# A spectral filter and a gated MLP on one core: real filter copied on chip, two row groups transposed by DMA, one input batch loaded in quarters

## The chip, the core and the metric

The kernel runs on one core of one Trainium2 chip. The time is the device time of one execution in microseconds; of several executions the median is given. A core has five engines with an instruction queue each: TensorE (PE, whose weight loads are listed as PEld), VectorE (DVE), ScalarE (ACT), GpSimd (POOL) and SyncE (SP). SyncE here does nothing but issue DMA transfers; GpSimd issues the loads of inputs and also computes. Matmuls write to PSUM, and another engine must copy ("evacuate") the result to SBUF before TensorE can use it again.

## What is computed

```python
X = np.fft.rfft(x, axis=1)              # x: 8 x 3008 x 256
Y = X * (filt_r + 1j * filt_i)[None]    # filters: 1505 x 256
y = np.fft.irfft(Y, n=3008, axis=1)
t = y.reshape(8 * 3008, 256)
h = t @ w_in                            # 256 -> 2048
g = h * sigmoid(beta * h)
out = g @ w_out                         # 2048 -> 256
```

A convolution along the sequence of each of eight batches, by Fourier transform, and then a two-layer network with a gated activation on all 24064 tokens. Inputs and output are float32; the kernel works in bfloat16 between them.

## The kernel before

The transform of length 3008 = 47 x 64 is done by matmuls with tables of sines and cosines, in four steps. Step 1 (`s1`, L628; for batch 0 `first1`, L305) transforms over the 47; `a` is its result. A transposition brings `a` into the tile `a2`. Step 2 (`s23`, L661) transforms over the 64, the spectrum is multiplied with the filter (L672 to L677, p_t, q_t and their sum v_t), and step 3 (L687) transforms back over the 64; the result `z` goes through DRAM (L692, L699) into tiles `zz` with the 96 rows in partitions. Step 4 (`last4`, L557) transforms back over the 47 and gives `y`. Batches 1 to 7 do all this with DMA transposes for `a2` (`a2_read`, L648: eight instructions of 128 x 768 on SyncE).

Batch 0 goes first, alone, in a stage of some 36 us in which the tables are made as well. There the filter is held doubled: `fri` has the real part in partitions 0 to 63 and the imaginary part in 64 to 127. `product(i)` makes two products for two frequencies, `inverse3(i)` runs two iterations behind it: eight matmuls into the PSUM tile `psz` (L477), evacuated into `z_t`. `z_t` holds 32 columns j in four groups of eight. Group 0 is transposed at once (L592), put through `last_z` (step 4 of batch 0), and the main stage begins. Groups 1 to 3 are transposed inside the main stage by `turn_z` (L549, eight transposes on TensorE into `pz`, then one evacuation into `zz`), two units for a group.

The main stage is a loop over 47 blocks of 512 tokens by 16 slices of the hidden layer, 752 steps. A step multiplies with a slice of w_in (L852, two matmuls of 512 columns into `hps`), has ScalarE evaluate the activation (L867) and, two steps later, multiplies with w_out (L907, four matmuls of 256 columns into `acc`). After 16 steps the block is copied from `acc` to `ost` and stored.

The Fourier work of the later batches, and the rest of batch 0, is strewn over these steps. The order is written by hand: `place(a, z, units)` spreads a list of small functions evenly over the steps a to z; at each step the functions placed there are emitted between its L852 and its L907 matmuls. Each engine and each DMA queue then works in that order. The lists that matter here are `uz(g)` (turn_z and last_z of group g), `u1(b)` (step 1), `u23(b)` (steps 2 and 3; 15 units, step 3 three units behind step 2), `u4(b)` (step 4), `ut` (a sign change of a table), `ux(b)` (load of a batch's x on the GpSimd queue) and `uf(a, z)`.

`uf` loads the filter's real part a second time, into both halves of `frr`, with 12 transfers on the SyncE queue: batches 1 to 7 multiply p_t with `frr` and q_t with the upper half of `fri`. The tile `frr` can't be filled earlier in its upper 16 rows of frequencies, because w_out is staged there (`load_wout`, L146) until `scale_wout` (L153, GpSimd) has brought it into `wout_sb`.

There are three PSUM pools: `hpsum` (two buffers), `opsum` and `fpsum` (three each). A PSUM tile's matmuls wait until the evacuation of the buffer's earlier content is done. `xpool` has one buffer, so the x of a batch can be loaded only after step 1 of the batch before.

Of the kernel before, what the change touches and what calls it, by code (L numbers as in the profile page):

```python
# [9 lines left out]
P = 128  # L10
# [3 lines left out]
F32 = mybir.dt.float32  # L14
BF16 = mybir.dt.bfloat16
# [11 lines left out]
M = 64  # L27
H = M // 2
NK = 24
J = 32  # L30
KG = 6
NG = NK // KG
JG = 8
NJG = J // JG
# [5 lines left out]
def kernel(  # L40
# [10 lines left out]
    nc = tc.nc  # L51
# [71 lines left out]

    X_WHOLE = [(0, 80, 0, J), (80, NP, 0, J)]
    X_HALVES = [(0, 80, 0, J // 2), (80, NP, 0, J // 2), (0, 80, J // 2, J), (80, NP, J // 2, J)]
    X_FIRST = [(0, 80, 0, JG), (80, NP, 0, JG), (0, 80, JG, 2 * JG), (80, NP, JG, J)]
    X_FIRST += [(0, 80, g * JG, (g + 1) * JG) for g in range(2, NJG)]

# [290 lines left out]
    xs = {}  # L419
# [14 lines left out]
    for go in tabs[::-1]:  # L434
        go()

    z_t = ypool.tile([P, NDC, J, KP], BF16, name="z_t", tag="y")
    pq = {}

    def product(i):  # L440
# [22 lines left out]
    def inverse3(i):  # L463
        k0 = 2 * i
        p_t, q_t = pq.pop(i)

        last = i == NK // 2 - 1
        for j0, j1 in ((0, JG), (JG, J)) if last else ((0, J),):
            nj = 4 * (j1 - j0)
            if j0:  # L470
                ps = fpsum.tile([P, 2, NDC, nj], F32, name="psz", tag="f")
            else:
                ps = opsum.tile([P, 2, NDC, nj], F32, name="psz", tag="acc")
            for src, tab in ((p_t, t3), (q_t, t3b)):
                for e in range(2):
                    for dc in range(NDC):
                        nc.tensor.matmul(  # L477
                            ps[:, e, dc, :],
                            lhsT=src[:, e, dc * P : (dc + 1) * P],
                            rhs=tab[:, k0 + e, 4 * j0 : 4 * j1],  # L480
                            start=src is p_t and dc == 0 and e == 0,
                            stop=src is q_t,
                            skip_group_check=True,
                        )
            for e in range(2) if last else (None,):
                if last:
                    dst = z_t[:, :, j0:j1, 4 * (k0 + e) : 4 * (k0 + e) + 4]
                    src = ps[:, e].rearrange("p c (j a) -> p c j a", a=4)
                else:
                    dst = z_t[:, :, :, 4 * k0 : 4 * k0 + 8].rearrange(  # L490
                        "p c j (e a) -> p e (c j) a", e=2
                    )
                    src = ps.rearrange("p e c (j a) -> p e (c j) a", a=4)
                evac(dst, src, not last or j0 > 0)

    def table4():
        for src, dst in ((t1b, t4b), (t1, t4)):
# [7 lines left out]
    for i in range(NK // 2 + FLAG):  # L505
# [24 lines left out]
        if i >= FLAG:  # L530
            inverse3(i - FLAG)

    for i in range(4):
        scale_wout(i)

    ys = {}
    ys[0] = ypool.tile([P, NDC, NK * P], BF16, name="y", tag="y")
    zz0 = {}
    zz0[0] = apool.tile([P, NK * P], BF16, name="zz", tag="a1")
    zz0[0] = zz0[0][:KP, : JG * D].rearrange("p (j d) -> p j d", j=JG)  # L540


    def turn_z(g, i, on_act=False):
        if g not in zz0:
            zz0[g] = zzpool.tile([KP, JG, D], BF16, name="zz", tag="zz")
        pz = fpsum.tile([P, 4, D], BF16, name="pz", tag="f")
        for e in range(4):
            for dc in range(NDC):
                nc.tensor.transpose(  # L549
                    pz[:KP, e, dc * P : (dc + 1) * P], z_t[:, dc, JG * g + 4 * i + e, :], ident[:]  # L550
                )
        evac(zz0[g][:, 4 * i : 4 * i + 4, :], pz[:KP], on_act)

    def last4(zz, tab, jj, dc, dst, on_act, own=None, first=NP):
        ps = own or fpsum.tile([P, 4, P], F32, name="ps4", tag="f")
        for e in range(4):
            nc.tensor.matmul(  # L557
                ps[:, e, :NP],
                lhsT=zz[:, jj + e, dc * P : (dc + 1) * P],
                rhs=tab[:],  # L560
                start=True,
                stop=True,
            )
        rest = []
        for n0, n1 in ((0, NP),) if own is None or first == NP else ((0, first), (first, NP)):
            rest.append(
                lambda n0=n0, n1=n1: evac(
                    dst[:, n0:n1],
                    ps[:, :, n0:n1].rearrange("p j n -> p n j"),
                    on_act,  # L570
                    inv_scale,
                )
            )
        rest.pop(0)()
        return rest
# [8 lines left out]

    for i in range(4):
        if i % 2:
            pz = opsum.tile([P, 2, D], BF16, name="pz", tag="acc")
        else:
            pz = fpsum.tile([P, 2, D], BF16, name="pz", tag="f")
        for e in range(2):  # L590
            for dc in range(NDC):
                nc.tensor.transpose(  # L592
                    pz[:KP, e, dc * P : (dc + 1) * P], z_t[:, dc, 2 * i + e, :], ident[:]
                )
        evac(zz0[0][:, 2 * i : 2 * i + 2, :], pz[:KP], i % 2 == 1)
    pw[0] = hpsum.tile([P, TB], F32, name="pw", tag="hps")
    warm(1)
    rest = []
# [23 lines left out]

    def s1(b, i, on_act):
        s = st[b]
        jq, dc = divmod(i, NDC) if b == 1 else divmod(i, J // 4)[::-1]
        ps = fpsum.tile([P, 4, P], F32, name="ps1", tag="f")
        for e in range(4):
            nc.tensor.matmul(  # L628
                ps[:, e, :KP],
                lhsT=s["x"][:, 4 * jq + e, dc * P : (dc + 1) * P],  # L630
                rhs=t1b[:],
                start=True,
                stop=True,
            )
        dst = s["a1"][dc].rearrange("p (k j a) -> p j k a", j=J, a=4)
        evac(
            dst[:, 4 * jq : 4 * jq + 4],
            ps[:, :, :KP].rearrange("p j (k a) -> p j k a", a=4),
            on_act,
        )  # L640
# [53 lines left out]
    def zz_read(b):  # L694
        s = st[b]
        s["zz"] = []
        for h in range(NJG):
            t = zzpool.tile([KP, JG, D], BF16, name="zz", tag="zz")
            nc.sync.dma_start(t[:], s["d2r"][:, h * JG : (h + 1) * JG, :])  # L699
            s["zz"].append(t)  # L700

    def s4(b, i, on_act):
# [37 lines left out]
    def u23(b):  # L740
        return [lambda i=i: s23(b, i) for i in range(NK // 2 + VLAG)]
# [2 lines left out]
        return [lambda i=i: s4(b, i, act and i % 2 == 1) for i in range(J // 2)]  # L744

    def uz(g, act=False):
        return [lambda i=i: turn_z(g, i) for i in range(2)] + [
            lambda i=i: last_z(g, i, act) for i in range(2 * NDC)
        ]

    def uf(a, z):
        return [
            go
            for k0 in range(a, z, JG)
            for at in (0, M)
            for go in load_filter(frr, filt_r, at, k0, JG, nc.sync)
        ]


    def ut(n):  # L760
# [4 lines left out]
            for k in range(0, NK, NK // n)  # L765
        ]

    def ux(b):
        def go():
            xs[b] = load_x(b, X_WHOLE)  # L770

        return [go]

    place(0, 0, rest, per=9)
    place(1, 14, uz(1, True))
    place(15, 29, uz(2, True))
    units = uz(3, True)
    place(20, 24, units[:2], per=2)
    place(34, 58, units[2:])

    first_step = [(S * b // TB) * NFB for b in range(B + 1)]
    if B > 1:
        units = u1(1, True)
        place(3, 8, units[: J // 4], per=2)
        place(10, 10, uf(0, JG), per=9)
        at = place(9, 14, units[J // 4 :], per=9)
        place(at + 1, at + 1, [lambda: a2_read(1)] + uf(JG, NK), per=9)
        place(14, 20, ut(4), per=2)
        units = u23(1)
        place(20, 53, units[: NK // 2], per=2)  # L790
        at = place(55, 58, units[NK // 2 :], per=2)
        assert at < 60
        place(60, 60, [lambda: zz_read(1)], per=9)
        place(67, 79, u4(1), per=2)
    if B > 2:
        place(36, 36, ux(2), per=9)
        at = place(52, 66, u1(2, True), per=3)
        assert at < 75
        place(75, 75, [lambda: a2_read(2)], per=9)
    for b in range(2, B):  # L800
# [38 lines left out]
    for s in range(len(steps) + LAG):  # L839
# [34 lines left out]
        if s >= LAG:  # L874
# [40 lines left out]
            if fb == NFB - 1:  # L915
                for h, a in enumerate(acc):
                    if h * per % 2 == 0:
                        ost = ostp.tile([P, 2, D], F32, name="ost", tag="ost")
                    c = h * per % 2
                    on_act = h == 0 and i < 6 or last and h == 0  # L920
                    if last and h == nch - 1:
                        for half in range(2):
                            cols = slice(half * P, (half + 1) * P)
                            evac(ost[:, c : c + per, cols], a[:, :, cols], half == 1)
                    else:
                        evac(ost[:, c : c + per, :], a[:], on_act)
                    store(t0 + h * per * P, per * P, ost[:, c : c + per, :])


# [28 lines left out]
```

## Time and profile before

| what | value |
|---|---|
| median of 5 runs | 776.81 us (776.61 to 779.73) |
| the profiled execution | 776.79 us |
| its span | 775.0 us |
| TensorE busy | 766.6 us |
| ScalarE busy | 595.5 us |
| VectorE busy | 378.9 us |
| GpSimd busy | 142.9 us |
| step 0's first L852 matmul starts at | 36.5 us |

The span is the time from the first to the last instruction in the trace; the device time is 1.8 us longer. Lines begin with the line number of the kernel where that is meant; in a line of instructions "out<-in" names the tile written and the tiles read, with partitions x elements and type. After the bar in a row of a group come its total busy time, the mean of one in ns, and the idle time of the engine just before, with what ended it. "xN" counts instructions. A queue's rows end in q (SPq).

### The profile page before, as it was taken

What the parts mean: (1) busy time and instruction counts of PE and PEld (TensorE: products, weight loads), DVE (VectorE), ACT (ScalarE), POOL (GpSimd) and SP (SyncE); (2) the same over time, 40 slices, a digit from 0 to 9 for tenths busy, and PEclk for the clock granted to TensorE, in tenths of its full rate; (3) what the DMA queues carried; (4) which work ended last, traced back from release to release, by engine and by line L of the source; (5) the groups of instructions that cost most, each with busy time, mean ns of one, the idle gap of its engine ahead of it and who ended that gap; (6) DMA issues with size and microseconds to landing.
All of it is one profiled execution on the core that took longest, in us unless ns stands there. A gap on an engine that the chain in (4) does not pass through costs nothing.

```text
span 775.0 us, 16219 instructions
## 1 busy us (share of the span) xinstructions
PE 766.6 (99%) x6444; PEld 553.8 (71%) x6444; DVE 378.9 (49%) x641; ACT 595.5 (77%) x926; POOL 142.9 (18%) x145
## 2 busy tenths in 40 slices
PE   8999999999999999999999999999999999999998
PEld 4877777777777777877778777787777776776665
DVE  7836846645446553474526735277353761401001
ACT  7888887886678867787677876778767787677776
POOL 7523401420013100231002410034000430000000
PEclk9999999999999999999999999999999999999999
DMA  7969755516911268022861237512451114100101
GB/s 177 237 159 195 167 162 112 135 49 156 175 43 69 92 142 161 30 92 80 157 134 50 75 120 142 106 66 78 130 110 55 49 69 129 56 28 28 55 28 55
DMA packets 103291, 80.48 MB, mean 104 GB/s; under 512 B 48466, under 2 KB 96996, under 8 KB 102258
## 3 DMA queue, kind: packets, MB, share of 16 engines
q1 hardware_dynamic: 100496, 63.73, 30.5%
q0 software_dynamic: 2720, 15.73, 10.6%
q8 instruction: 50, 0.82, 0.4%
q14 instruction: 25, 0.20, 0.1%
HBM read 46.15 MB, written 35.65 MB: 106 GB/s over the span
## 4 chain that ended last, share of the span: by engine, by line
PE 97%; ACT 1%; DMA 1%; DVE 0%; POOL 0%; issue 0%; POOLq 0%; DVEq 0%
PE acc L907 42%; PE hps L852 42%; PE ps L557 3%; PE ps L628 3%; PE ps L687 2%; PE ps L661 2%; DMA xg<-in_x_dram 1%; PE psz L477 1%; PE pz L549 0%; ACT a L109 0%; ACT a_t L109 0%; PE pb L403 0%; POOL xg L120 0%; PE ps L451 0%; PE ps2q L451 0%
## 5 line engine op out<-in xcount | busy, mean ns | idle before, releaser
L867 ACT ACTIVATE gT<-hps,beta_sb 128x512 bf16<-128x512 f32 x752 | 516.5, 688 | 166.5 <-PE hps L852 154.9
L907 PE MATMUL acc<-wout_sb,gT 128*128 128x256 bf16 x3008 | 451.5, 272 | 0.0
L852 PE MATMUL hps<-y,win_sb 128*128 128x512 bf16 (+8 forms) x1730 | 447.7, 351 | 0.0
L907 PEld LDWEIGHTS <-gT 128*128 128x128 bf16 x3008 | 279.6, 98 | 106.3 <-ACT gT L867 0.2
L852 PEld LDWEIGHTS <-win_sb 128*128 128x128 bf16 x1730 | 165.0, 98 | 24.4 <-issue 0.2
L677 POOL TENSOR_TENSOR v_t<-p_t,q_t 128x512 bf16<-128x512 f32 x84 | 106.8, 1271 | 383.9 <-DVE q_t L676 375.3
L111 DVE COPY ost<-acc 128x512 f32<-128x512 f32 (+2 forms) x89 | 56.6, 675 | 194.1 <-PE acc L907 188.4
L111 DVE CAST a<-ps 128x384 bf16<-128x384 f32 x96 | 53.5, 558 | 91.5 <-PE ps L628 91.4
L113 DVE TENSOR_SCALAR y<-ps 128x376 bf16<-128x376 f32 (+1 forms) x115 | 61.7, 545 | 59.5 <-PE ps L557 59.5
L672 DVE TENSOR_TENSOR p_t<-ps,frr 128x512 f32<-128x512 f32 x84 | 58.1, 692 | 33.4 <-PE ps L661 30.9
L676 DVE TENSOR_TENSOR q_t<-ps,fri 64x512 f32<-64x512 f32 x84 | 58.3, 694 | 1.2
L673 DVE SCALAR_TENSOR_TENSOR q_t<-ps,fri 64x512 f32<-64x512 f32 x84 | 57.4, 684 | 1.1
L557 PEld LDWEIGHTS <-zz 96*128 96x128 bf16 x512 | 35.3, 97 | 29.1 <-issue 0.3
L109 ACT ACTIVATE z<-ps 128x512 bf16<-128x512 f32 x84 | 49.7, 591 | 0.0
L628 PEld LDWEIGHTS <-xg 94*128 94x128 bf16 x448 | 30.7, 97 | 23.6 <-issue 0.6
L628 PE MATMUL ps<-t1b,xg 94*128 94x96 bf16 x448 | 36.7, 205 | 0.1
L557 PE MATMUL ps<-t,zz 96*128 96x94 bf16 x448 | 36.7, 204 | 0.0
L661 PE MATMUL ps<-a,t 128*128 128x256 bf16 x168 | 32.1, 273 | 0.0
L687 PE MATMUL ps<-v_t,t 128*128 128x256 bf16 x168 | 32.1, 273 | 0.0
L120 POOL DMA_DIRECT2D xg<-in_x_dram x22 | 12.1, 552 | 98.0 <-PE acc L907 93.9
L661 PEld LDWEIGHTS <-t 128*128 128x128 bf16 x168 | 15.7, 98 | 14.1
L687 PEld LDWEIGHTS <-t 128*128 128x128 bf16 x168 | 16.3, 98 | 6.4 <-DVE q_t L676 0.4
(118 smaller groups left out, 192.7 us busy)
## 6 DMA issues: line engine op xcount, KB each, us to landing
out_dram<-ost SPq DMA_DIRECT2D x80, 256.0 KB
d<-z SPq DMA_DIRECT2D x28, 384.0 KB
zz<-d SPq DMA_DIRECT2D x28, 384.0 KB
xg<-in_x_dram POOLq DMA_DIRECT2D x6, 1280.0 KB, 10.2
frr<-in_filt_r_dram SPq DMA_DIRECT2D x12, 256.0 KB
out_dram<-ost SPq DMA_DIRECT2D x20, 128.0 KB
frr<-in_moe_w_out_dram POOLq DMA_DIRECT2D x4, 512.0 KB, 13.0
xg<-in_x_dram POOLq DMA_DIRECT2D x6, 224.0 KB, 11.1
```

The lines of the kernel that those rows point to most:

```text
L111: nc.vector.tensor_copy(dst, src)
L113: nc.vector.tensor_scalar_mul(dst, src, scale)
L557: nc.tensor.matmul(ps[:, e, :NP], lhsT=zz[:, jj + e, dc * P : (dc + 1) * P], rhs=tab[:], start=True, stop=True,)
L628: nc.tensor.matmul(ps[:, e, :KP], lhsT=s["x"][:, 4 * jq + e, dc * P : (dc + 1) * P], rhs=t1b[:], start=True, stop=True,)
L661: nc.tensor.matmul(ps[:, e, :], lhsT=t2[:, k0 + e, 3:5, :].rearrange("p c k -> p (c k)"), rhs=s["a2"][g][:, :, kk + e, :], start=True, sto ...
L672: nc.vector.tensor_tensor(p_t[:], ps[:], frr[:, ks_, :], ALU.mult)
L676: nc.vector.tensor_tensor(q_t[:M], ps[M:P], fri[M:P, ks_, :], ALU.mult)
L677: nc.gpsimd.tensor_tensor(v_t[:], p_t[:], q_t[:], ALU.add)
L687: nc.tensor.matmul(ps[:, e, :], lhsT=t3[:, k0 + e, :], rhs=v_t[:, e, :], start=True, stop=True)
L852: nc.tensor.matmul(hps[:, pos - t0 : pos - t0 + ln], lhsT=win_sb[:, dc, fb * P : (fb + 1) * P], rhs=ys[b][:, dc, n0 : n0 + ln], start=(dc ...
L867: nc.scalar.activation(gT[:, :tn], hps[:, :tn], ACT.Silu, scale=beta_sb[:, fb : fb + 1])
L907: nc.tensor.matmul(acc[tb // per][:, tb % per, :], lhsT=g_[:, tb * P : (tb + 1) * P], rhs=wout_sb[:, f_, :], start=(f_ == 0 and tb % per = ...
```

## The change

- The upper half's copy of the real filter no longer comes from DRAM. GpSimd copies `fri[:64]` into both halves of `frr`, eight frequencies at a time (`double`): four copies behind `scale_wout`, two at steps 24 and 29. `uf` and its 12 transfers are gone.
- `z_t` is split. Group 0 has a tile of its own, `z_0`; groups 1 to 3 are in `z_t` in the order group, column half, j, row, with the rows padded from 96 to 128 by zeros. `inverse3` evacuates both pieces, so ten of the evacuations on ScalarE become two each.
- Groups 2 and 3 are turned by `read_z`: one DMA transpose each, of 128 x 2048, on the SyncE queue at step 9. Group 1 keeps `turn_z`, with its two evacuations on ScalarE instead of VectorE. `zz` tiles are laid out by column half first. The last_z units of groups 2 and 3 stand at steps 17 to 29 and 36 to 56.
- The x of batch 2 is loaded in quarters (two transfers each) at steps 29 to 41, not whole at step 36; step 1 of batch 2 stands at steps 56 to 69 instead of 52 to 66, in the order of batch 1.
- The last 128 tokens: each half of the columns gets a tile of its own and its own store, one issued by SyncE and one by ScalarE.

```diff
-    z_t = ypool.tile([P, NDC, J, KP], BF16, name="z_t", tag="y")
+    z_0 = a2pool.tile([P, NDC, JG, KP], BF16, name="z_0", tag="a2")
+    z_t = ypool.tile([P, NJG - 1, NDC, JG, P], BF16, name="z_t", tag="y")
+    gp.memset(z_t[:, :, :, :, KP:], 0.0)
...
-            for e in range(2) if last else (None,):
-                if last:
-                    dst = z_t[:, :, j0:j1, 4 * (k0 + e) : 4 * (k0 + e) + 4]
-                    src = ps[:, e].rearrange("p c (j a) -> p c j a", a=4)
-                else:
...
-                evac(dst, src, not last or j0 > 0)
+            for e0, ne in ((0, 1), (1, 1)) if last else ((0, 2),):
+                cols = slice(4 * (k0 + e0), 4 * (k0 + e0 + ne))
+                if j0 == 0:
+                    evac(
+                        z_0[:, :, :, cols].rearrange("p c j (e a) -> p e (c j) a", a=4),
+                        ps[:, e0 : e0 + ne, 0].rearrange("p e c (j a) -> p e (c j) a", a=4),
+                        not last,
+                    )
+                if j1 == J:
+                    evac(
+                        z_t[:, :, :, :, cols].rearrange("p g c j (e a) -> p e (g c j) a", a=4),
...
+    def double(k0, at):
+        gp.tensor_copy(frr[at : at + M, k0 : k0 + JG, :], fri[:M, k0 : k0 + JG, :])
+
     for i in range(4):
         scale_wout(i)
+    for k0 in (0, JG):
+        for at in (0, M):
+            double(k0, at)
...
+    def read_z(g):
+        zz0[g] = zzpool.tile([P, NDC, JG, P], BF16, name="zz", tag="zz")
+        nc.sync.dma_start_transpose(
+            zz0[g].rearrange("p c j d -> p (c j) d"),
+            z_t[:, g - 1].rearrange("p c j r -> p (c j r)"),
+        )
...
-        jq, dc = divmod(i, NDC) if b == 1 else divmod(i, J // 4)[::-1]
+        jq, dc = divmod(i, NDC) if b < 3 else divmod(i, J // 4)[::-1]
...
-    place(1, 14, uz(1, True))
-    place(15, 29, uz(2, True))
-    units = uz(3, True)
-    place(20, 24, units[:2], per=2)
-    place(34, 58, units[2:])
+    place(9, 9, [lambda: read_z(2), lambda: read_z(3)], per=9)
+    place(1, 14, [lambda i=i: turn_z(1, i, True) for i in range(2)] + uz(1, True))
+    place(17, 29, uz(2, True))
+    place(36, 56, uz(3))
...
-        place(10, 10, uf(0, JG), per=9)
         at = place(9, 14, units[J // 4 :], per=9)
-        place(at + 1, at + 1, [lambda: a2_read(1)] + uf(JG, NK), per=9)
+        place(at + 1, at + 1, [lambda: a2_read(1)], per=9)
         place(14, 20, ut(4), per=2)
+        place(24, 29, [lambda at=at: double(2 * JG, at) for at in (0, M)], per=9)
...
-        place(36, 36, ux(2), per=9)
-        at = place(52, 66, u1(2, True), per=3)
+        place(29, 41, ux(2, X_QUARTERS), per=9)
+        at = place(56, 69, u1(2, True), per=3)
...
-                        for half in range(2):
+                        for half, eng in ((0, nc.sync), (1, nc.scalar)):
                             cols = slice(half * P, (half + 1) * P)
-                            evac(ost[:, c : c + per, cols], a[:, :, cols], half == 1)
-                    else:
-                        evac(ost[:, c : c + per, :], a[:], on_act)
+                            ost = pqpool.tile([P, 2, D], F32, name="ost", tag="pq"[half] + "_t")
+                            evac(ost[:, :1, :P], a[:, :, cols], half == 1)
+                            eng.dma_start(out[TOK - P :, cols], ost[:, 0, :P])
+                        continue
+                    evac(ost[:, c : c + per, :], a[:], on_act)
```

## The prediction

> **What bounds the kernel now.** I read the page's head first, then its chain of waits.
>
> ```profile
> span 775.0 us, 16219 instructions
> PE 766.6 (99%) x6444; PEld 553.8 (71%) x6444; DVE 378.9 (49%) x641; ACT 595.5 (77%) x926; POOL 142.9 (18%) x145
> PE 97%; ACT 1%; DMA 1%; DVE 0%; POOL 0%; issue 0%; POOLq 0%; DVEq 0%
> ```
>
> TensorE is busy 766.6 of 775.0 us and is 97% of the chain that ended last. So a deleted TensorE instruction shortens the run by its own spacing, and everything done on other engines is free until TensorE has to wait for it. I then read the chain in order of time where the change acts (start, length, what).
>
> ```profile
> 53.69 0.43 PE hps L852 x2
> 54.12 0.45 PE pz L549 x8
> 54.57 0.44 PE acc L907 x4
> ...
> 56.30 0.45 PE pz L549 x8
> ...
> 58.92 0.43 PE hps L852 x2
> 59.52 0.45 PE pz L549 x8
> ...
> 64.05 0.45 PE pz L549 x8
> ```
>
> The transposes of batch 0's groups 2 and 3 (turn_z, L549) stand in the chain itself, 0.45 us for a unit of 8. A step without extra work is 0.43 + 0.44 = 0.87 us.
>
> Third, the stretch before step 0, 5 us at a time (columns: stretch, length, then busy us and count of PE, PEld, DVE, ACT, POOL, the granted clock, DMA share, GB/s):
>
> ```profile
> 20.00:25.00 5.00, 4.90 (x73) 4.71 (x73) 4.22 (x8) 4.83 (x9) 2.64 (x6) 1.00 1.02 231
> 25.00:30.00 5.00, 5.00 (x74) 4.59 (x72) 5.00 (x10) 4.21 (x8) 3.58 (x6) 1.00 1.04 172
> ```
>
> Here PE, DVE and ACT are all nearly full: no engine has much to give. Fourth, the waits of the Sync queue and the rows of its transfers:
>
> ```profile
> 46.29 0.23 SPq L521 DMA_DIRECT2D mark<-xg  x1
> ...
> 52.66 12.04 SPq L648 DMA_TRANSPOSE a<-a  x8
> ...
> L648 SPq DMA_TRANSPOSE a<-a x56: 1210/1287/6620, 52.7 to 578.4; - x56
> ```
>
> The second is the reading of batch 1's a2 by DMA transposes; the third gives least, median and most ns of one such instruction over all batches.
>
> **The change part by part.**
>
> *Transposes removed from TensorE.* In the instruction order 32 transposes with their weight loads are gone: turn_z of groups 2 and 3, four units. 4 x 0.45 = **-1.8 us**, all on the path. Their four evacuations of 0.69 us leave VectorE, which was not on the path.
>
> *DMA transposes in their place.* Two instructions on Sync, each of 128 x 2048 elements, 16 blocks of 128 x 128. No row has this size. The nearest, L648, moves 6 blocks in 1.21 to 1.29 us: 0.213 us a block, 16 x 0.213 = 3.4 us each, 6.8 us for both. Group 2 is first used in step 17 (about 57 us), group 3 in step 36. The Trainium skill speaks against this: "VectorE: DVE Perf Modes", section "The three transpose paths", puts a 128 x 128 bf16 block at 390 ns on TensorE and 1309 ns by the DMA crossbar. By that, one instruction is 16 x 1.309 = 20.9 us, both 41.9 us, and batch 1's transposes, behind them on the queue, would be some 35 us late: a run near 810 us. The row is of the same operation on the same queue and gives a sixth of that price per block when blocks share an instruction (and TensorE's block costs 0.056 us in the chain, not 0.39), so I take the row.
>
> What is queued behind them decides. Sync issues them after the mark (46.29 + 0.23 = 46.52), so they end at 46.5 + 6.8 = 53.3. Batch 1's eight transposes began at 52.66 and now begin at 53.3. The first two make the tile that the first L661 matmul reads: 53.3 + 2 x 1.28 = 55.9, and the transfer share falls to 0.00 within about 0.9 us of the last issue of such a group (125.1, batch 2), so it lands near 56.8. TensorE reaches that matmul in step 20, one step number earlier than before: 58.92 + 0.43 - 2 x 0.45 (two units gone by then) + 0.17 (one last_z unit now ahead of it) = 58.6. Margin 1.8 us. Each group of eight has one instruction of about 2.0 to 2.3 us, 1 us over the median; two such would use the margin up. I put +0.1 us here, from 0 to 5 (the upper end below, as a rival). The rows near 6.6 us come from stretches where an x load runs beside them; between 46.5 and 56 none is left, since the filter loads are gone.
>
> *Filter reload removed.* 12 Sync transfers of 256 KB and their issue go (4 before the transposes, 8 after at 64.88 to 68.7); output stores behind them move up by 4 us. TensorE waited for none of this: 0 us.
>
> *GpSimd copies.* Six of 64 x 2048 f32. Not in the trace. By element, the bf16 copy L293 (768 in 0.83 us) gives 2.2 us, the multiplication L153 (1024 in 1.89 us) 3.8 us; I take 3, nearer to a copy. Four run after the last L153 (44.27 + 1.89 = 46.2) and end at 55 to 61.4; the first v_t was at 63.28. The other two stand between v_t adds from step 24 on and delay one by at most 3.8 us, with 8 us before its matmul. 0 us, hidden behind the steps' matmuls. If the first four exceed (69.4 - 1.3 - 46.2) / 4 = 5.5 us each, the first L687 matmul at 69.40 waits, 4 us for each us more. VectorE is under 60% busy there, so VectorE slowed by the copies would stay covered.
>
> *More instructions on ScalarE before step 0.* z_t is split: each of the ten whole evacuations in inverse3 becomes two, of 128 and 384 elements. Rows:
>
> ```profile
> L109 ACT ACTIVATE z_t<-psz 128x512 bf16<-128x512 f32 x11 | 6.4, 595 | 1.2 <-PE psz L477 1.2
> L109 ACT ACTIVATE a<-ps 128x384 bf16<-128x384 f32 x16 | 7.9, 492 | 0.0
> L109 ACT ACTIVATE t<-pt 128x128 bf16<-128x128 bf16 x1 | 0.3, 273 | 0.0
> ```
>
> 492 + 273 - 595 = 170 ns by durations, but instructions overlap: starts lie 0.51 us apart behind a 512, 0.37 behind a 384, 0.16 to 0.22 behind a 128, so +0.02 to +0.08. "VectorE: DVE Perf Modes", section "The TRN2 errata", has a fixed 172 cycles at 1.2 GHz for a PSUM source, 143 ns a split: 0.86 us over the six iterations in which ScalarE also evacuates a table or an a2. By the row it is 0.1 to 0.5, which pushes back the full TensorE and VectorE behind it. Against it, group 0's transposes now wait for the small piece of the last evacuations, not the whole (0.51 + 0.595 against 0.57 + 0.275: 0.26 us sooner). Net **+0.15**, between -0.2 and +0.9. The z_t memset on GpSimd (1536 elements, up to 1.7 us) falls into a wait of 1.78 us for a filter load.
>
> *Group 1's evacuations go to ScalarE.* Two of 96 x 1024, about 1.05 us by the slope of the rows, near 38.6 and 40.7. ScalarE had a gap of 1.38 us before the silu of step 4. The psum buffer of the second comes free at about 41.8, and the matmuls that need it stood at 42.1. 0 us, at most +0.3.
>
> *Batch 2's x in quarters and its later s1.* Eight GpSimd issues of 0.55 us instead of two, +3.3 us on an engine that is 18% busy; they land before step 56. s1 has the same 64 matmuls, moved among full steps: 0 us.
>
> *The last store.* Both halves get tiles of their own and two queues. The profile's tail is:
>
> ```profile
> 771.35 0.29 DVE L111 COPY ost<-acc 128x128 f32<-128x128 f32 x1 [0.34 <-PE acc L907]
> 771.67 0.28 ACT L109 ACTIVATE ost<-acc 128x128 f32<-128x128 f32 x1 [1.14 <-DVE ost L111]
> ...
> 771.98 0.41 SPq L812 DMA_DIRECT2D out_dram<-ost  x1
> ```
>
> ScalarE's half still waits for VectorE's in the new order, so its store is issued at 772.0 as before; only 64 KB less follow it. **-0.1**, from +0.1 to -0.4.
>
> Sum: -1.8 + 0.1 + 0.15 - 0.1 = -1.65 us. The profiled execution took 776.79 us (span 775.0 and 1.8 around it), the median of five is 776.81, so the sum carries over: 776.81 - 1.65 = **775.2 us**.
>
> **The rivals.**
> 1. *Small gain, as summed*, 774.5 to 776.5: chance 0.57. That is under 0.3% (2.3 us), about what a measurement tells from no change.
> 2. *Nothing is lost*: split free, 0.26 us earlier into step 0, tail at its best: -1.8 - 0.2 - 0.4 = -2.4, 774.4 us; with transposes a little dearer than 0.45 (a wait or a buffer that goes with them) 774.0. For it: PE never waits for long. Against: ScalarE is full at 20 to 25 us. Chance 0.22.
> 3. *The wait for a2 takes the place of the transposes*, slower. Place: the first L661 matmul in step 20, in-order on TensorE. If the pair of DMA transposes takes more than 6.8 + 1.8 = 8.6 us, each further us is one us of run; from 10.3 us (5.1 each) on the kernel is slower than before. At the 6.62 us of the longest row, 13.2 us, the stall is 4.6: 776.8 - 1.7 + 4.6 = 779.7. For it: sixteen blocks in one instruction are not in the trace, and rows of up to 6.62 us for six blocks are. Chance 0.15, of which 0.13 clearly slower.
> 4. *GpSimd copies too slow*: at 7 us each the first L687 waits 6 us, 781 us. Against: both nearby rows. Chance 0.05.
> 5. *The change doesn't do what it says*: no effect, 776.8. Nearly excluded, since the deleted units are in the chain. 0.01.
>
> **How the numbers follow.** Faster by over 0.3% (below 774.5): rival 2, 0.22. Slower by over 0.3% (above 779.1): 0.13 of rival 3 and rival 4, 0.18. The rest, 0.60. The likeliest case alone spans 774.5 to 776.5. To hold 8 in 10 the range takes in rival 2's 774.0 and rival 3 up to a stall of 4 us: 779.0.
>
> **What would show it.** Right: L549 with 16 transposes; no PE wait on the L661 group; the two new transfers about 3.4 us each on Sync and batch 1's from about 53.3; the six copies 2.2 to 3.8 us; TensorE's busy time 1.8 us lower. Wrong: PE idle behind a DMA near 58 us (rival 3), or behind v_t near 69 us (rival 4); step 0 starting more than 0.5 us later than 36.5 (ScalarE mis-sized).

## The result, and the profile after

| | before | after |
|---|---|---|
| median | 776.63 us (775.79 to 779.73, 48 runs) | 775.19 us (774.54 to 776.15, 26 runs) |
| profiled execution | 776.79 us | 774.61 us |
| its span | 775.0 us | 772.8 us |
| step 0's first matmul into `hps` starts at | 36.55 us | 36.07 us |
| from there to the end of the span | 738.45 us | 736.73 us |

The medians lie 1.44 us apart where 1.65 were forecast (775.2). The ratio of the executions is 0.9979, with a 95% interval of 0.9974 to 0.9984, that is 1.2 to 2.0 us less. The change is measurable over this many runs and under the 0.3% that was taken as the limit of one measurement. The profiled pair differs by 2.2 us, more than the medians. Of that, 1.72 us lie behind step 0 (last row of the table) and 0.48 ahead of it, and 0.29 of the 0.48 are there before the first product of `inverse3` (20.10 and 19.81 us).

The head of the page and the shares of the chain of waits, after:

```profile
span 772.8 us, 16168 instructions
PE 764.6 (99%) x6412; PEld 552.3 (71%) x6412; DVE 376.7 (49%) x639; ACT 595.9 (77%) x935; POOL 158.5 (21%) x158
PE 97%; ACT 1%; DVE 1%; issue 0%; POOL 0%; DVEq 0%; POOLq 0%
```

TensorE still bounds the kernel. It is busy 2.0 us less with 32 instructions fewer, and the 1% of the chain that DMA held before is gone. The chain in order of time, at step 0 and at step 20 (start, length, what):

```profile
36.07 1.02 PE hps L867 x6
37.09 0.45 PE pz L568 x8
...
57.47 0.53 PE hps L867 x2
58.00 0.22 PE ps L683 x2
58.22 0.43 PE acc L922 x4
```

`turn_z` (now L568) is in the chain for group 1 alone. The first matmul on batch 1's a2 (now L683) follows the `hps` pair of step 20 directly. From step 0 to that pair it is 21.40 us, and was 22.37: 0.97 less, for the two units gone by then. The transfers of SyncE (start, length, count) and the group row of the new ones (least, median and most ns of one, first and last start):

```profile
43.80 0.23 SPq L533 DMA_DIRECT2D mark<-xg  x1
44.22 4.13 SPq L573 DMA_TRANSPOSE zz<-z_t  x2
51.94 12.08 SPq L670 DMA_TRANSPOSE a<-a  x8
L573 SPq DMA_TRANSPOSE zz<-z_t x2: 1962/2034/2107, 44.2 to 46.4; - x2
```

The two hold the queue 2.03 us each, until 48.35. The queue then stands 3.59 us before batch 1's can begin, so they delay nothing. The new groups on GpSimd and ScalarE (busy, mean ns, idle before):

```profile
L547 POOL COPY frr<-fri 64x2048 f32<-64x2048 f32 x6 | 11.3, 1888 | 0.2
L109 ACT ACTIVATE z_t<-psz 128x384 bf16<-128x384 f32 x11 | 5.5, 503 | 0.0
L109 ACT ACTIVATE zz<-pz 96x1024 bf16<-96x1024 bf16 x2 | 2.1, 1028 | 0.0
```

The stretch before step 0 (columns as before: stretch, length, busy us of PE, PEld, DVE, ACT, POOL with counts, clock, DMA share, GB/s) and the tail:

```profile
20.00:25.00 5.00, 5.00 (x78) 4.82 (x76) 4.94 (x10) 4.89 (x13) 4.88 (x9) 1.00 1.06 227
25.00:30.00 5.00, 4.95 (x70) 4.41 (x68) 4.75 (x9) 4.34 (x11) 2.88 (x4) 1.00 1.06 198
```

```profile
769.07 0.29 DVE L111 COPY ost<-acc 128x128 f32<-128x128 f32 x1 [0.40 <-PE acc L922]
769.40 0.28 ACT L109 ACTIVATE ost<-acc 128x128 f32<-128x128 f32 x1 [1.21 <-DVE ost L111]
769.64 0.41 SPq L941 DMA_DIRECT2D out_dram<-ost  x1
```

The two stretches are as full as they were. In the tail ScalarE's half still waits for VectorE's, and the span ends 3.1 us behind this store (772.8 - 769.71, ScalarE's issue beside it); before it was 3.0 (775.0 - 771.98).

### The profile page after: what moved, and what is told of

It reads as the page before. It is cut to its first block, busy times and chain, and to the rows that moved or that the text cites. A ratio compares the mean times of both kernels' runs of the same rounds, so it can differ in the third digit from the quotient of the medians.

```text
span 772.8 us, 16168 instructions
## 1 busy us (share of the span) xinstructions
PE 764.6 (99%) x6412; PEld 552.3 (71%) x6412; DVE 376.7 (49%) x639; ACT 595.9 (77%) x935; POOL 158.5 (21%) x158
## 4 chain that ended last, share of the span: by engine, by line
PE 97%; ACT 1%; DVE 1%; issue 0%; POOL 0%; DVEq 0%; POOLq 0%
PE acc L922 43%; PE hps L867 42%; PE ps L581 3%; PE ps L650 2%; PE ps L683 2%; PE ps L709 2%; PE psz L481 1%; ACT a L109 0%; PE pb L404 0%; ACT a_t L109 0%; ACT t L281 0%; ACT r L285 0%; PE ps L455 0%; DVE qb_t L464 0%; PE ps2q L455 0%
## 5 line engine op out<-in xcount | busy, mean ns | idle before, releaser
L113 DVE TENSOR_SCALAR y<-ps 128x376 bf16<-128x376 f32 (+1 forms) x119 | 63.9, 545 | 60.2 <-PE ps L581 60.1
L120 POOL DMA_DIRECT2D xg<-in_x_dram x28 | 15.3, 550 | 98.2 <-PE acc L922 93.8
L683 PE MATMUL ps<-a,t 128*128 128x256 bf16 x168 | 32.1, 273 | 0.0
L683 PEld LDWEIGHTS <-t 128*128 128x128 bf16 x168 | 15.9, 98 | 15.1
```

The costliest lines, as they stand in the source:

```text
L113: nc.vector.tensor_scalar_mul(dst, src, scale)
L683: nc.tensor.matmul(ps[:, e, :], lhsT=t2[:, k0 + e, 3:5, :].rearrange("p c k -> p (c k)"), rhs=s["a2"][g][:, :, kk + e, :], start=True, sto ...
```

## The experiments

Theory: the gain is the 32 transposes and everything else lies beside TensorE. Rival: the gain is something else (the filter's transfers, the store), or the transposes' gain is partly eaten by ScalarE's extra instructions or by a late a2. Each ratio below is to the kernel before, on the same chip. "The changed kernel" has the ratio 0.9979.

### Groups 2 and 3 on TensorE again

```diff
-    place(9, 9, [lambda: read_z(2), lambda: read_z(3)], per=9)
...
-    place(17, 29, uz(2, True))
+    place(15, 29, [lambda i=i: turn_z(2, i) for i in range(2)] + uz(2, True))
+    place(20, 24, [lambda i=i: turn_z(3, i) for i in range(2)], per=2)
```

> The changed kernel with groups 2 and 3 turned by TensorE again (32 transposes back, evacuated by VectorE, at the steps of the kernel before); copies, split, quarters and store stay. Theory (the 1.8 us of L549 in the chain are the gain): 1.8 us slower than the changed kernel, so 775.19 + 1.8 = 777.0 us, 0.3 to 0.4 us above the kernel before. Rival (the gain comes from the other edits, such as the filter that no longer loads the queues): still near 775.2 us.

Measured: 776.23 us (775.82 to 780.17, 11 runs), ratio 0.9996 [0.9983, 1.0009]; span 774.7 us. 777.0 had been expected; by the two ratios some 1.3 us of 1.8 come back. The traces show it more closely, in one execution each: from step 0 to the last copy from `acc` to `ost` the changed kernel takes 1.79 us less than the kernel before, and this one 0.11 us less, so 1.68 us come back. In the main stage TensorE waits for nothing new. So the gain is that of the transposes. Nothing is seen of the rest of the change together; the interval of this ratio leaves it between -1.3 and +0.7 us.

### The last store, and the split evacuations, by themselves

The changed kernel with the old store:

```diff
-                        for half, eng in ((0, nc.sync), (1, nc.scalar)):
+                        for half in range(2):
...
-                            ost = pqpool.tile([P, 2, D], F32, name="ost", tag="pq"[half] + "_t")
-                            evac(ost[:, :1, :P], a[:, :, cols], half == 1)
-                            eng.dma_start(out[TOK - P :, cols], ost[:, 0, :P])
-                        continue
-                    evac(ost[:, c : c + per, :], a[:], on_act)
+                            evac(ost[:, c : c + per, cols], a[:, :, cols], half == 1)
+                    else:
+                        evac(ost[:, c : c + per, :], a[:], on_act)
```

> The changed kernel with the last store of the kernel before (one transfer for both halves, one tile). My sum: 0.1 us slower, 775.3 us; from the two traces, in which span's end lies 3.0 and 3.1 us behind the last issue, rather 0.0. Rival (the store by a second queue is a gain or a loss of its own): 775.5 or more, or 775.0 or less.

Measured: 774.76 us (774.48 to 775.34, 9 runs), ratio 0.9977 [0.9968, 0.9987]. The new store gains nothing that can be measured.

The kernel before with `z_t` split into `z_0` and `z_t` and each whole evacuation made two, as in the change, and nothing else:

```diff
+    z_0, z_t = z_t[:, 0], z_t[:, 1:]
...
-                evac(dst, src, not last or j0 > 0)
+                if j0 == 0:
+                    evac(
+                        z_0[:, :, :, cols].rearrange("p c j (e a) -> p e (c j) a", a=4),
+                        ps[:, e0 : e0 + ne, 0].rearrange("p e c (j a) -> p e (c j) a", a=4),
+                        not last,
+                    )
+                if j1 == J:
+                    evac(
+                        z_t[:, :, :, :, cols].rearrange("p g c j (e a) -> p e (g c j) a", a=4),
...
```

> The kernel before with one edit: ScalarE evacuates the ten whole psz tiles in two pieces of 128 and 384 elements, into a z_t laid out by groups; nothing else. My sum: +0.15 us (step 0 later by -0.2 to +0.9), so 776.8 us. By the fixed 143 ns for each more instruction that the Trainium skill's table gives: +0.86 us on step 0, 777.5. In the trace the first L852 matmul should start within 0.2 us of 16.45 us behind the first psz matmul.

Measured: 776.43 us (776.02 to 778.78), ratio 0.9998 [0.9988, 1.0007]. By the interval, ten more instructions on ScalarE in its fullest stretch cost between -0.9 and +0.5 us. The trace can say more. From the first `psz` matmul (20.32) to step 0 (36.55) it is 16.23 us, against 16.45 in the kernel before, and in the traces of all the kernels with the split it is 16.23 to 16.26. So the split costs nothing there, and step 0 comes 0.2 us earlier with it; of the kernel before there is one trace. (The 778.78 us of the profiled execution hold a wait of TensorE of 1.9 us for an x load at 95 us, far behind step 0.)

### More DMA transposes ahead of a2

Two further transposes of the same size behind the first two, into a tile that nothing reads; a second kernel has six (`range(6)`):

```diff
+    def again():
+        t = zzpool.tile([P, NDC, JG, P], BF16, name="zz", tag="zz")
+        for i in range(2):
+            nc.sync.dma_start_transpose(
+                t.rearrange("p c j d -> p (c j) d"),
+                z_t[:, 1 + i % 2].rearrange("p c j r -> p (c j r)"),
+            )
...
-    place(9, 9, [lambda: read_z(2), lambda: read_z(3)], per=9)
+    place(9, 9, [lambda: read_z(2), lambda: read_z(3), again], per=9)
```

> The changed kernel with two more DMA transposes of 128 x 2048 into an unused tile right behind the two of step 9, ahead of batch 1's eight on the same queue. At the 2.03 us measured for one, SyncE is through with four at 44.2 + 8.1 = 52.3, about when batch 1's could start anyway (51.94). Theory (margin): 775.2 us as the changed kernel. Rival (transposes cost the run something whatever their place): 0.3 us or more slower.

> The same with six more: eight transposes take to 44.2 + 16.2 = 60.4, batch 1's start 8.5 us later than in the changed kernel. Its first two land about 3.5 us after that, 63.9, and the first matmul on a2 stood at 58.0. Theory (the wait for a2, one us of run for each us past the margin): TensorE idle about 5.9 us there, 781 us. If the step order absorbs it: less than 777.

Measured: with two 774.53 us (774.38 to 777.42), ratio 0.9981 [0.9967, 0.9994], no cost. With six 790.66 us (790.18 to 791.69), ratio 1.0177 [1.0153, 1.0201]. SyncE with two more:

```profile
44.80 4.07 SPq L573 DMA_TRANSPOSE zz<-z_t  x2
48.92 5.41 SPq L794 DMA_TRANSPOSE zz<-z_t  x2
54.42 11.59 SPq L670 DMA_TRANSPOSE a<-a  x8
```

SyncE with six more, and the wait and the first matmul on a2 of TensorE in that kernel:

```profile
44.52 3.70 SPq L573 DMA_TRANSPOSE zz<-z_t  x2
48.27 20.11 SPq L794 DMA_TRANSPOSE zz<-z_t  x6
```

```profile
72.40 0.60 PE L683 MATMUL ps<-a,t 128*128 128x256 bf16 x2 [14.06 <-DMA a<-a]
```

This is rival 3 with its price, and it gives the margin. The a2 transposes began at 68.46 and the matmul came 3.94 us later. In the changed kernel they begin at 51.94, so by the same 3.94 us a2 is there near 55.9. The matmul starts at 57.84 in the timeline (the chain above counts it from the end of the pair ahead of it, 58.00): an estimated 1.96 us to spare, and 3.59 us of idle queue ahead of that. The pair could take 4.13 + 3.59 + 1.96 = 9.7 us before TensorE waits. With two more that margin is used up to 0.15 us (54.42 + 3.94 = 58.36, matmul at 58.51) and nothing is lost, with six it is overrun. The size expected for six was wrong in two terms. First, the six held the queue 20.11 us and not 12.2. The transposes themselves took no longer than the 2.03 us assumed. But `again` writes all of them into one tile, so each has to wait until the one before it has landed. SyncE's wait (us in total, times, longest) and the six instructions (least, median and most ns):

```profile
SPq L794 <- DMA zz<-z_t: 10.2, 5, 2.2
L794 SPq DMA_TRANSPOSE zz<-z_t x6: 1395/1589/1947, 48.3 to 67.0; - x6
```

Five waits of some 2 us make 10.2 of the 20.11 us. The 5.41 us of the two further transposes hold one such wait of 2.2 us. Neither row says how long the queue is held by transposes that have a tile each; that a2 comes late by what the queue is held, and what this costs, stands.

Second, 14.1 us of waiting made the kernel 16.1 us slower than with two. A lower clock goes with it: the granted clock is 0.66 at 60 to 65 us and 0.50 from there to 75 us. TensorE works again from 72.40 on, and half speed until 75.3 costs some 1.4 of the other 2 us (more on this in the last section).

### Group 1 by DMA as well

Three attempts at going further. The first issues all three transposes in step 0 and leaves the mark out:

```diff
-    place(9, 9, [lambda: read_z(2), lambda: read_z(3)], per=9)
-    place(1, 14, [lambda i=i: turn_z(1, i, True) for i in range(2)] + uz(1, True))
+    place(0, 0, [lambda: read_z(1), lambda: read_z(2), lambda: read_z(3)], per=19)
+    place(6, 14, uz(1, True))
...
-                mark3 = dpool.tile([1, D], BF16, name="mark3", tag="mark3")
-                nc.sync.dma_start(mark3[:], xs[1][:1, J - 1, :])
```

> The changed kernel with group 1 turned by a DMA transpose too: the mark that held the SyncE queue until batch 1's x had landed is left out, and three transposes are issued in step 0; 16 more TensorE transposes and two ScalarE evacuations go. Theory: 2 x 0.45 = 0.9 us faster than the changed kernel, 774.3 us, if group 1 lands before step 6 (about 42.5). Rival (with w_out and x loading beside them the transposes take 4 to 6.6 us each, and group 1 is late): 775 to 780 us, with TensorE waiting at the first matmul on group 1's tile.

Measured: 780.85 us (780.16 to 783.11), ratio 1.0053 [1.0032, 1.0074]. Its SyncE, and TensorE's wait:

```profile
35.26 13.09 SPq L571 DMA_TRANSPOSE zz<-z_t  x3
```

```profile
46.66 0.47 PE L579 MATMUL ps<-t4b,zz 96*128 96x94 bf16 x4 [4.13 <-DMA zz<-z_t]
```

The three are not alike (least, median and most ns):

```profile
L571 SPq DMA_TRANSPOSE zz<-z_t x3: 1870/1975/9154, 35.3 to 46.5; - x3
```

The first, which is group 1's, holds the queue 9.15 us beside the loads of w_out and x (DMA share 1.09 at 40 to 45 us), the others 1.98 and 1.87. The "4.4 us" of the expectation below is the mean of the three and fits none of them. TensorE's wait is not the whole loss either: it works at a granted clock of 0.50 from 46.66 to 52.2, which costs some 2.8 us more. The second attempt keeps the mark ahead of them:

```diff
-    place(9, 9, [lambda: read_z(2), lambda: read_z(3)], per=9)
-    place(1, 14, [lambda i=i: turn_z(1, i, True) for i in range(2)] + uz(1, True))
+    place(9, 9, [lambda: read_z(1), lambda: read_z(2), lambda: read_z(3)], per=9)
+    place(12, 15, uz(1, True))
```

> The changed kernel with row group 1 turned by a third DMA transpose as well, issued behind the mark together with the other two and ahead of them (it takes the place of 16 TensorE transposes and two ScalarE evacuations; the first uses of group 1 move from steps 3 to 14 to steps 12 to 15). If a DMA transpose behind the mark takes its 2.03 us and sits in the stretch in which the queue idles before 51.9 us, TensorE loses 2 x 0.45 us and nothing waits: 0.9 us under the changed kernel, about 774.3 us, and the three transposes end near 50.4. If the third one lands after step 12 (about 49 us) or runs at the 4.4 us that it took beside the loads of w_out, TensorE waits for it on L581 and the time is 775 to 780.

Measured: 775.84 us (774.02 to 778.39, 11 runs), ratio 0.9985 [0.9971, 1.0000]. TensorE's wait:

```profile
51.16 0.33 PE L581 MATMUL ps<-t4b,zz 96*128 96x94 bf16 x4 [1.15 <-DMA zz<-z_t]
```

The transposes begin at 45.33 there and take 7.60 us for the three:

```profile
L573 SPq DMA_TRANSPOSE zz<-z_t x3: 1830/2147/3519, 45.3 to 51.1; - x3
```

Again the first, group 1's, is the long one, 3.52 us; why it is longer than the first of a pair (2.11) is not known. The group is late by 1.15 us, more than the 0.9 that was to be gained. The third puts its first uses at the end:

```diff
-    place(12, 15, uz(1, True))
+    place(14, 15, uz(1, True), per=2)
```

> The kernel in which group 1 too is turned by a DMA transpose behind the mark, with the four first uses of group 1 at steps 14 and 15, two a step, and not at 12 to 15. There TensorE stood 1.15 us on L581 for the transposed group, until 51.16 us; step 14 begins near 52.3. If the transpose lands as there, the wait is gone and the time is 0.9 us under the changed kernel, 774.3 us; if ScalarE's four evacuations of y in two steps are too much ahead of step 16, a wait of some tenths on hps or y takes part of it; if nothing is won, about 775.2.

Measured: 774.71 us (774.13 to 775.33, 6 runs), ratio 0.9972 [0.9960, 0.9983]; span 772.3 us. The wait is gone. The median is 0.5 us under that of the changed kernel, but the intervals overlap, so it isn't shown to be faster. From step 0 to step 20's `hps` it takes 21.16 us, against 21.40: of 0.9 us only 0.24 arrive by then. One place of the loss can be seen at the start:

```profile
37.68 0.59 PE L867 MATMUL hps<-y,win_sb 128*128 128x512 bf16 x2 [0.34 <-ACT gT L882]
```

Where `turn_z` of group 1 stood at step 1, TensorE now waits 0.34 us for the first activation: that unit had been filling a gap. The other 0.3 stay open. From step 0 to the end of the span it is 736.0 us against 736.7, so at the end some 0.7 are there, in one execution each; what brings the part behind step 20 is open too.

### x of batch 2 whole

```diff
-        jq, dc = divmod(i, NDC) if b < 3 else divmod(i, J // 4)[::-1]
+        jq, dc = divmod(i, NDC) if b == 1 else divmod(i, J // 4)[::-1]
...
-        place(29, 41, ux(2, X_QUARTERS), per=9)
-        at = place(56, 69, u1(2, True), per=3)
+        place(36, 36, ux(2), per=9)
+        at = place(52, 66, u1(2, True), per=3)
```

> The changed kernel with batch 2's x loaded whole at step 36 and its step 1 at steps 52 to 66 in the old order. Theory (moved among full steps, costs nothing): 775.2 us, within 0.3. Rival (the quarters are part of the gain): 775.6 or more.

Measured: 775.26 us median, but 774.34 to 782.37: five of twelve executions lie above 777.5, where the highest of 26 of the changed kernel is 776.15. (Of the kernel before, executed beside this one, four of 23 lie there, so the spread need not be this kernel's own.) Ratio 0.9997 [0.9975, 1.0019]. The profiled execution took 780.73. ScalarE and then TensorE in it:

```profile
91.89 0.60 ACT L109 ACTIVATE z<-ps 128x512 bf16<-128x512 f32 x1 [4.78 <-DMA d<-z]
```

```profile
93.11 1.01 PE L867 MATMUL hps<-y,win_sb 128*128 128x512 bf16 x2 [4.01 <-ACT gT L882]
```

ScalarE stands 4.78 us before an evacuation into a `z` buffer that an earlier transfer to DRAM still holds; the activations stand behind it in order, and TensorE stops. In the one execution seen this is what a late transfer does. That the quarters are what prevents it, or that every slow execution has this cause, is not shown; the median says that the quarters gain nothing, the spread leaves room for their keeping something off.

### The filter reloaded

The changed kernel with the twelve transfers in place of the six copies:

```diff
-    for k0 in (0, JG):
-        for at in (0, M):
-            double(k0, at)
...
+        place(10, 10, uf(0, JG), per=9)
...
-        place(at + 1, at + 1, [lambda: a2_read(1)], per=9)
+        place(at + 1, at + 1, [lambda: a2_read(1)] + uf(JG, NK), per=9)
...
-        place(24, 29, [lambda at=at: double(2 * JG, at) for at in (0, M)], per=9)
```

> The changed kernel with the filter's real part loaded a second time by 12 SyncE transfers as before, instead of GpSimd's six copies; the DMA transposes stay ahead of them. Theory (no engine waited for the loads): 775.2 us, within 0.4. If the loads are what would make the DMA transposes late, as in the rival of the wait for a2: the two transposes longer than 2.1 us each or batch 1's later than 53, and TensorE idle at the first matmul on a2 in step 20; each us idle is one us of run, up to 5.

Measured: 779.34 us (777.22 to 781.83, 12 runs), ratio 1.0031 [1.0017, 1.0045]: 4.2 us over the changed kernel and slower than the kernel before, which has the same twelve transfers. VectorE in this kernel:

```profile
76.62 0.69 DVE L111 COPY ost<-acc 128x512 f32<-128x512 f32 x1 [3.10 <-DMA out_dram<-ost]
77.34 0.69 DVE L691 TENSOR_TENSOR p_t<-ps,frr 128x512 f32<-128x512 f32 x1
...
78.74 0.69 DVE L695 TENSOR_TENSOR q_t<-ps,fri 64x512 f32<-64x512 f32 x1
79.46 0.55 DVE L113 TENSOR_SCALAR y<-ps 128x376 bf16<-128x376 f32 x1
```

TensorE in it:

```profile
79.49 0.39 PE L706 MATMUL ps<-v_t,t 128*128 128x256 bf16 x2 [2.40 <-DVE q_t L695]
```

The stores of `out` stand behind the reload on the queue; a copy into `ost` waits 3.10 us for one of them. Behind that copy stand, in order, the filter products and the evacuation of a `y` of group 3. They hold two of `fpsum`'s three buffers, and TensorE stops. This trace is of a quick execution, 777.45 us, and its wait of 2.40 us accounts for what that one lost. Five of the twelve executions lie at 777.2 to 777.6 us, with a mean granted clock of 0.999 or more; the other seven at 779.2 to 781.8, six of them with 0.995 to 0.998. So half of the executions had a lower clock besides the wait, as the last section shows it in a trace. The kernel before has the same late store, with VectorE standing 2.44 us, and TensorE doesn't stop. VectorE and ScalarE of the kernel before:

```profile
77.29 0.69 DVE L111 COPY ost<-acc 128x512 f32<-128x512 f32 x1 [2.44 <-DMA out_dram<-ost]
```

```profile
75.48 0.49 ACT L109 ACTIVATE y<-ps 128x376 bf16<-128x376 f32 x1
```

Two readings were tested: the quarters of x meet the reload, or the `y`, which the change moves from ScalarE to VectorE (`uz(3, True)` became `uz(3)`), is what uncovers it. First the reload with x whole, that is with the x load and the step 1 of batch 2 of the kernel before:

```diff
-        place(29, 41, ux(2, X_QUARTERS), per=9)
-        at = place(56, 69, u1(2, True), per=3)
+        place(36, 36, ux(2), per=9)
+        at = place(52, 66, u1(2, True), per=3)
```

> The changed kernel with the filter reloaded by twelve transfers and x of batch 2 whole at step 36, its step 1 from 52 to 66: the transfers of the kernel before, with the two DMA transposes and the new evacuations. The loss of the kernel with the reload alone (779.3 us) was seen as VectorE standing 3.1 us before a copy into ost, whose store was late, with TensorE waiting 2.4 us behind it. If it takes the reload and the quarters of x from step 29 together, this kernel loses only what the kernel before does (its VectorE stands 2.4 us at the same place and TensorE does not wait): about 775.2 us. If the reload alone is enough once the DMA transposes stand ahead of it, the time is again 778 to 780 and TensorE waits on L706 near 77 us.

Measured: 779.04 us (776.83 to 780.89, 11 runs), ratio 1.0024 [1.0010, 1.0038]. The quarters are not it. Then the reload with the quarters, and group 3's evacuations back on ScalarE:

```diff
-    place(36, 56, uz(3))
+    place(36, 56, uz(3, True))
```

> The kernel with the filter reloaded by twelve transfers (779.3 us), with one thing put back besides: the four evacuations of row group 3 between steps 36 and 56 go to ScalarE, as in the kernel before, and not to VectorE. The reading to be tested: in the kernel with the reload VectorE stands 3.1 us before a copy into ost whose store is late; behind that copy stand p_t, q_t and the evacuation of y of group 3, so two of the three PSUM buffers that step 3's products share stay taken and TensorE stops on L706. The kernel before has the same stand of VectorE (2.4 us), but its y goes through ScalarE at 75.5 us and TensorE goes on. If that is the cause, TensorE doesn't wait near 77 us here, and the time is 775.2 to 775.8, though VectorE still stands some 3 us. If the late store is enough by itself, 778 to 780 again with the wait on L706.

Measured: 776.17 us (774.39 to 778.05, 11 runs), ratio 0.9990 [0.9978, 1.0002]. VectorE, ScalarE and TensorE in it:

```profile
78.68 0.69 DVE L111 COPY ost<-acc 128x512 f32<-128x512 f32 x1 [3.08 <-DMA out_dram<-ost]
```

```profile
76.74 0.47 ACT L109 ACTIVATE y<-ps 128x376 bf16<-128x376 f32 x1
```

```profile
78.02 0.38 PE L706 MATMUL ps<-v_t,t 128*128 128x256 bf16 x2
```

VectorE stands as long as it did, the `y` passes on ScalarE, and L706 doesn't wait there (at its next use, 81.55, it waits 0.32 us). This one argument gives back 3.2 of the 4.2 us. The last 1.0 us is not settled: this kernel's executions spread from 774.4 to 778.1, and the profiled one shows short waits of TensorE for loads (0.8 us for an a2, 0.5 for an x). The kernel before with nothing but this move of the `y` was not run.

## Why the prediction was right

The time was forecast at 775.2 us and is 775.19. The mechanism was right: 32 transposes leave a full TensorE, and what replaces them fits beside it. The closeness to 0.01 us is luck. The base was taken 0.18 us too high (776.81 of five executions, 776.63 of 48) and the gain 0.21 us too large (1.65 for 1.44), and the two cancel. Inside the sum the three small terms were all off. Step by step:

- *Transposes removed, -1.8.* Right. The main stage became 1.72 us shorter, 0.97 of it by step 20, when two of the four units are gone. With the units back on TensorE 1.68 us are lost again.
- *DMA transposes, 3.4 us each, batch 1's from 53.3.* The mechanism held, the term was mis-sized: 2.03 us each, batch 1's from 51.94, and the +0.1 put down for a late a2 is 0. The margin, forecast at 1.8 us with the queue running through, is 1.96 and an idle 3.59 us ahead of it. Scaling L648's row by blocks was too dear, since a block of a larger instruction held the queue for less: 0.127 us of 16 against 0.213 of 6. The price from "The three transpose paths" in "VectorE: DVE Perf Modes", 20.9 us each, is seen in no run; the dearest was 9.15, beside loads. Another page of the Trainium skill was nearer: "DMA: Bandwidth & Descriptors", section "Latency and other measured facts", gives 261 GB/s for DMA transposes with a non-contiguous middle dimension in one kernel, and 350 to 400 for contiguous ones. For 128 x 2048 x 2 bytes = 524 kB the first is 2.0 us, and 2.03 us is 258 GB/s.
- *Filter reload removed, 0.* This step failed, though the sum doesn't show it. It was read from the kernel before, where the late store is covered. The change takes the cover away: the move of group 3's `y` evacuations from ScalarE to VectorE was in the diff and was not costed at all. Together the two are worth nothing that can be measured. Beside a reload the move costs some 3 us: 779.34 us with the `y` on VectorE and 776.17 with it on ScalarE. The removal is therefore not idle in the changed kernel.
- *GpSimd copies, 3 us each.* 1.89 us, below the lower bound of 2.2. The four end at 43.52 + 7.71 = 51.23, and the first `v_t` is at 60.57: 0 us, as forecast.
- *Split evacuations, +0.15.* From the first `psz` to step 0 it is 16.26 us, and was 16.45: -0.19, and -0.22 with the split alone. The lower end of the range, -0.2, was the right one. But the reason forecast for it, group 0's transposes waiting for a smaller piece, is not what the traces show: their wait is 0.19 us with and without the split. The largest difference lies ahead of them, where TensorE waits 0.66 us for `qb_t` in the kernel before and 0.21 with the split alone; what makes it is open. The 0.86 us worked out from "The TRN2 errata" of "VectorE: DVE Perf Modes" isn't there.
- *Group 1's evacuations on ScalarE, 0.* Right: 1.03 us each (1.05 forecast), no wait behind them.
- *Quarters of x, 0.* Right for the median; what they do to the spread is open.
- *Last store, -0.1.* It is 0, by the tail and by the old store put back.
- *Rivals.* Rival 2 ("nothing is lost", 774.0 to 774.4) came true in two of its parts, the split and the a2, but not in the tail (0 for -0.4) nor in its time: 775.19. The profiled pair is 2.2 us apart; the medians hold 0.8 less. Start times differ from one execution to the next (step 0 begins at 36.0 to 36.9 us in the profiled executions of the kernels with the changed setup), so one pair can't settle that. Rival 3 has its place and mechanism right, its threshold at 9.7 us and not 8.6, and its price of one us per us too low for a long wait (16.1 for 14.1). Rival 4's threshold was not reached.

## What to carry to other kernels

To take work off a full TensorE, turn tiles by DMA in a stretch where the queue idles and no load runs, and work out how late the next transfer on that queue may be: the answer here is the margin that two further transposes used up and six overran. Give every transpose a tile of its own when its cost is to be measured; with one tile for all, the wait for the landing is measured as well. Before a removed transfer is booked at nothing, look for evacuating engines that stand before a late store, and ask which of the change's small moves of an evacuation puts a shared PSUM buffer behind them. An instruction that goes from a step with a latency to hide (the first steps of a pipeline) may have been filling a gap, and then gives nothing.

## What the runs showed of the hardware

A DMA transpose of 128 x 2048 bf16 holds the SyncE queue for less time than it needs to land. In the changed kernel the pair holds it 2.11 and 1.96 us. Where each transpose had to wait for the one before it to land, an instruction held it 1.40 to 1.95 us, and the starts lay 3.7 us apart (from 52.23 to 66.97; 4.0 for the one right behind the pair): that is about the time from start to landing. The first of three was longer, 3.52 us in the second attempt on group 1 and 9.15 us beside the loads of w_out and x in the first. So a row gives a cost only for similar company, and a mean over unlike instructions gives none.

A long wait of TensorE costs more than its length. The stretches behind the wait of 2.80 us in the kernel with reload and whole x (the number behind the five engines is the granted clock):

```profile
78.00:80.00 2.00, 0.00 (x0) 0.00 (x0) 1.97 (x3) 0.00 (x0) 0.00 (x0) 1.00 0.24 80
80.00:82.00 2.00, 1.84 (x8) 1.14 (x9) 1.93 (x4) 0.60 (x1) 1.73 (x2) 0.57 0.68 264
82.00:84.00 2.00, 2.00 (x9) 1.10 (x8) 0.79 (x2) 0.69 (x1) 1.60 (x3) 0.57 0.98 131
```

In finer stretches of the same trace the clock stands at 0.50 from 80.3 to 83.7, some 1.7 us of work lost in 3.4. Behind the wait of 2.40 us in the kernel with the reload it stays at 1.00. The three other traces in which it falls in the main stage have it at 0.50 for 3.4 us (x whole, a wait of 4.01), for 6.8 (45.4 to 52.2, first attempt on group 1, 4.13) and for 13.7 (61.6 to 75.3, six more transposes, 14.06): once, twice and four times 3.4 us. "TensorE: Matmul & The Clock Gate", section "HAM oscillation", warns of idle gaps over some 3.4 us; here one of 2.80 was enough and one of 2.40 was not, in one execution each. A rival that is a wait should have this in its price.
